# Fourteen unread products ahead of each pair's products with v, and earlier ScalarE copies, in the first stage of an attention and mixing kernel

## The chip, the core and the metric

The kernel runs on one core of one Trainium2 chip. The metric is the device time of one execution in microseconds (us). The core has five engines that run side by side, each through its own list of instructions in order: TensorE (PE, with its weight loads as PEld), VectorE (DVE), ScalarE (ACT), GpSimd (POOL) and SyncE (SP), which issues the transfers. An instruction starts when the one before it on its engine lets it and when the results that it needs are there.

## The reference

Two steps for 8 batches of 576 tokens. First attention with 8 heads of 64 columns, in a causal window of 128 and with a bias that falls with distance; then a block that turns each value by an angle, mixes over the tokens and then over the channels.

```python
scores = scale * np.matmul(q, k.transpose(0, 1, 3, 2))
scores = np.where((rel >= 0) & (rel < 128), scores + bias[None], -1000000000.0)
attn = np.exp(scores - np.max(scores, axis=-1, keepdims=True))
attn = attn / (np.sum(attn, axis=-1, keepdims=True) + 1e-09)
x = concat_heads(np.matmul(attn, v))
theta = x @ w_theta
zr, zi = x * np.cos(theta), x * np.sin(theta)
y = np.einsum('ts,bsd->btd', w_tok_r, zr) + np.einsum('ts,bsd->btd', w_tok_i, zi)
u = x + y
out = u + np.maximum(u @ w_ch, 0.0)
```

## The kernel before

Heads go in pairs, so a batch has four pairs and the kernel 32. A pair passes through these steps. `scores` lets PE make the scores of five tiles in three groups into PSUM (`ps`, two buffers, and `mm`, four buffers); DVE adds the bias and takes the extreme (`weigh`, L433), and ScalarE takes the exponentials (L436). One half of a pair's weights is called `front`, the other `back`. `flip` turns a half so that the keys come to the partitions. For the first four pairs (`PLAIN`) PE turns eight blocks into PSUM and ScalarE copies them out (`pt`, L445). Later pairs are split into two half-precision parts, `hl`, by ScalarE (L450) and DVE (L452), and a transfer turns them (L454). `values` makes the products with v (`ps<-vb,pt` or `ps<-vh,pt`), and `finish` divides by the sums (L483 to L490) into `x_sb`.

The first stage is `start`: pairs 0 to 4, where the scores of a new pair stand between the two flips and the products with v of the pair before. In the same stage ScalarE and DVE unpack the weights (L168 to L193), which arrive as double-precision words, and DVE takes the largest v of each head (L258) and works out scales from it (`spread`, L268 to L288, with two small products on PE). Only pairs 0 to 3 have their products with v in `start`; pair 4 belongs to batch 1.

Then `turn` works out the angles of batch 0: PE turns `x_sb`, ScalarE and DVE cut it into two parts (`x_hi`, `x_lo`), PE multiplies by w_theta (`mm<-wth_hi,x_hi`), and ScalarE and DVE take sine and cosine and split the results (`z_hi` L512, `z_lo` L513). After that `attend` runs the pairs of batch 1 between the token products of batch 0 (`mix`), then `turn` of batch 1 comes, and so on to batch 7.

The order on each engine is fixed when the kernel is built: a scheduler places the instructions by its own picture of time, by the dependencies and by priorities. `tc.high_priority(FINISH)` lets what stands in it go sooner in that order. `tc.issue_after(x)` adds a dependency on x. From the first mix on, PE's products are kept in the order in which they are written (`pinned`); in `start` and `turn` they are not. SP's transfers are ordered by the same scheduler.

Of the kernel before, what the change touches and what calls it, by code (L numbers as in the profile page):

```python
# [11 lines left out]
F32 = mybir.dt.float32  # L12
# [4 lines left out]
BF16 = mybir.dt.bfloat16  # L17
# [16 lines left out]
STEPS, FINISH = ((7, 7, 6, 3), (3, 4, 6, 4), (3, 4, 6, 3)), 250  # L34

GROUP = 4
PLAIN = 4
RINGS = ([("mx", 2 * NT, 4)] + [("den", 2 * NT, 3)] + [("whole", 1, 2), ("vs", 2 * GROUP, 2), ("scale", 2 * GROUP, 2)]
         + [("whole0", 1, 1), ("vs0", 13, 1), ("scale0", 13, 1), ("sum", 9, 1),
# [10 lines left out]
def attn_moe_kernel(ctx: ExitStack, tc: tile.TileContext, qt, kt, vx, wth, wtok, wch, band, out):  # L50
    nc = tc.nc
# [16 lines left out]
    ps_m = ctx.enter_context(tc.tile_pool(name="ps_m", bufs=4, space=PSUM))  # L68
# [3 lines left out]
    def mm(*args, **kw):  # L72
        ins = nc.tensor.matmul(*args, **kw)  # L73
        if pinned:
            tc.keep_in_program_order(ins)

    def behind_all(some):
        stack = ExitStack()
        for ins in some:
            stack.enter_context(tc.issue_after(ins.ins))  # L80
        return stack
# [5 lines left out]
    def flipped(*args):  # L87
        ins = nc.tensor.transpose(*args)  # L88
        if pinned:
            tc.keep_in_program_order(ins)  # L90
# [19 lines left out]
    ident = fixed[:, :128]  # L110
# [16 lines left out]
    sums, rows, invs, lim = (rings[name].take() for name in ("sum", "row", "inv", "lim"))  # L127

    qr = const.tile([128, S + 64], F32, name="qr")
    second = vbp.tile([128, GROUP, NT, 65], F32, name="vb").rearrange("p h c d -> p (h c d)")  # L130
    qr_too, kr_too = second[:, :S + 64], second[:, S + 64:2 * S + 64]
# [110 lines left out]
    def load_plain(g):  # L242
        b, h = divmod(GROUP * g, H)
        vb = vbp.tile([128, GROUP, NT, 65], F32, name="vb")
        nc.sync.dma_start(out=vb, in_=vx[b, h:h + GROUP].rearrange("h p (c d) -> p h c d", d=65))
        return vb
# [3 lines left out]
    def load_values(g):  # L250
        b, h = divmod(GROUP * g, H)
        vb = vbp.tile([128, GROUP, NT, 65], F32, name="vb")
        nc.sync.dma_start(out=vb, in_=vx[b, h:h + GROUP].rearrange("h p (c d) -> p h c d", d=65))
        group_v[g] = vb

    def measure(g, to):

        return nc.vector.tensor_reduce(out=to, in_=group_v[g][:, :, :, :64], axis=mybir.AxisListType.XY, op=ALU.max,  # L258
                                       apply_absolute_value=True)
# [32 lines left out]
    def coming(b):  # L292
        return [g for g in (2 * b + 3, 2 * b + 4) if g < B * H // GROUP]
# [16 lines left out]
    def clamp_first():  # L310
        nc.vector.tensor_scalar(out=peaks[0][:, :H], in0=peaks[0][:, :H], scalar1=2.0 ** -100, scalar2=None,
                                op0=ALU.max)
# [72 lines left out]
    class Pair:  # L385


        def __init__(self, p):
            self.p = p
            self.terms = parts.pop(p)  # L390
            self.early = p < PLAIN
            self.heads = [Head(2 * p + e, self) for e in range(2)]
# [4 lines left out]
        def scores(self, tiles, behind=None):  # L397

            last = len(self.terms) - 1
            if tiles == (0,):  # L400
                _, _, k0, kn, _ = TILES[0]
                ps = ps_m.tile([128, 512], F32, name="mm")
                for j, (qm, km) in enumerate(self.terms):
                    mm(ps[:, :kn], qm[:, 512:], km[:, k0:k0 + kn], start=(j == 0), stop=(j == last))
                self.weigh(0, 0, self.src[0][:, :kn], ps[:, :kn], bands[:, 512:], behind)
                return
            ps = ps_s.tile([128, 2, 512], F32, name="ps")
            if tiles == (1, 2):
                sbs = [self.src[0][:, 256 + 384 * e:640 + 384 * e] for e in range(2)]
            else:  # L410
                self.src[1] = sp.tile([128, 1024], F32, name="back")
                sbs = [self.src[1][:, 512 * e:512 + 512 * e] for e in range(2)]
            off = 0
            for i in tiles:
                q0, qn, k0, kn, _ = TILES[i]
                for j, (qm, km) in enumerate(self.terms):
                    for e in range(2):
                        rows = slice(64 * e, 64 * e + 64)
                        mm(ps[:, e, off:off + kn], qm[rows, q0:q0 + qn], km[rows, k0:k0 + kn],
                                         start=(j == 0), stop=(j == last))  # L420
                off += kn
            off = 0
            for i in tiles:
                _, _, _, kn, c0 = TILES[i]
                for e in range(2):
                    sb = sbs[e][:, off:off + kn]
                    self.weigh(i, e, sb, ps[:, e, off:off + kn], bands[:, 256 * e + c0:256 * e + c0 + kn], behind)
                off += kn
# [9 lines left out]
        def flip(self, half):  # L438
            src = self.src[half]
            if self.early:  # L440
                t_ps = ps_s.tile([128, 2, 512], F32, name="ps").rearrange("p a c -> p (a c)")
                for n in range(8):
                    flipped(t_ps[:, 128 * n:128 * n + 128], src[:, 128 * n:128 * n + 128], ident)
                pt = ptp.tile([128, 1024], F32, name="pt")
                self.copied = nc.scalar.copy(pt, t_ps)  # L445
                parts_of = [pt]
            else:
                hl = hlp.tile([128, 2, 1024], F16, name="hl")
                pt = ptp.tile([128, 2, 1024], F16, name="pt")
                self.copied = nc.scalar.activation(hl[:, 0], src, AF.Copy, scale=2.0 ** PEXP)  # L450
                copied.append(self.copied)
                self.lowered = nc.vector.scalar_tensor_tensor(out=hl[:, 1], in0=src, scalar=2.0 ** PEXP, in1=hl[:, 0],  # L452
                                                              op0=ALU.mult, op1=ALU.subtract)
                nc.sync.dma_start(out=pt.rearrange("p a (n c) -> p (a n) c", c=128),  # L454
                                  in_=hl.rearrange("p a c -> p (a c)"), transpose=True)
                parts_of = [pt[:, a] for a in range(2)]
            for n, (i, e, j) in enumerate(TURNS[half]):
                for to in ((0, 1) if i == 0 else (e,)):
                    at = 128 * n + (64 * to if i == 0 else 0)
                    self.pt[i, to, j] = [t[:, at:at + 128] for t in parts_of]  # L460
# [217 lines left out]
    def prepare(p):  # L678

        if 0 <= p - 1 < pairs and p - 1 not in parts:  # L680
            parts[p - 1] = split_pair(p - 1, raw.pop(p - 1))
        if p < pairs and p not in raw:
            raw[p] = load_pair(p)
# [5 lines left out]
    def attend(b, x_sb, mixing, chans, first, behind, lowered):  # L689

        for g in range(H // 2):
# [15 lines left out]
            for tiles in SCORES:  # L707
                scores(tiles)
# [40 lines left out]
    def start(x_sb, load):  # L749

        paces = [0]

        def pace(k=1):
            for _ in range(k):
                paces[0] += 1
                if paces[0] * 2 % 5 < 2:
                    next(load, None)

        next(load)
        prepare(0)  # L760
        nc.sync.dma_start(out=bands, in_=band)
        prepare(1)
        last = None
        for p in range(H // 2 + 1):
            new = Pair(p)
            if p == 3:
                load_values(2)

            def scores(tiles):
                new.scores(tiles)  # L770
                pace(2 * len(tiles))

            if last is not None:
                last.flip(0)
                scores(SCORES[0])
                scores(SCORES[1])
                last.flip(1)
                scores(SCORES[2])
                last.values()
                with tc.high_priority(FINISH):  # L780
                    last.finish(x_sb)
            else:
                for tiles in SCORES:
                    scores(tiles)
            if p == 3:
                clamp_first()
            if p < H // 2:
                for head in new.heads:
                    head.ready()
            if p in (1, 2):  # L790
                measure(p - 1, peaks[0][:, GROUP * (p - 1):GROUP * p])
            prepare(p + 2)
            last = new
        for _ in load:
            pass
        for g in coming(0):
            load_values(g)
        return last
# [94 lines left out]
```

## Time and profile before

| what | value |
|---|---|
| median of the runs shown | 655.22 us (653.53 to 655.68, 3 runs) |
| the profiled execution's own time | 654.73 us |
| its span from the first to the last instruction | 652.7 us |
| mean granted clock of PE | 0.963 of full speed |
| PE busy | 604.9 us, 93% |
| DVE busy | 529.3 us, 81% |
| ScalarE busy | 499.0 us, 76% |

The span and the execution's own time differ by 2.03 us, which lie around the instructions. The busy shares are means over the whole span; the first stage differs from the rest, so it has to be read by itself. [...]

### The profile page before, as it was taken

What the parts mean: (1) busy time and instruction counts of PE and PEld (TensorE: products, weight loads), DVE (VectorE), ACT (ScalarE), POOL (GpSimd) and SP (SyncE); (2) the same over time, 40 slices, a digit from 0 to 9 for tenths busy, and PEclk for the clock granted to TensorE, in tenths of its full rate; (3) what the DMA queues carried; (4) which work ended last, traced back from release to release, by engine and by line L of the source; (5) the groups of instructions that cost most, each with busy time, mean ns of one, the idle gap of its engine ahead of it and who ended that gap; (6) DMA issues with size and microseconds to landing.
All of it is one profiled execution on the core that took longest, in us unless ns stands there. A gap on an engine that the chain in (4) does not pass through costs nothing.

```text
span 652.7 us, 14918 instructions
## 1 busy us (share of the span) xinstructions
PE 604.9 (93%) x5712; PEld 520.5 (80%) x5712; DVE 529.3 (81%) x1313; ACT 499.0 (76%) x945; POOL 145.7 (22%) x196
## 2 busy tenths in 40 slices
PE   4869888689999999999999999999999999999998
PEld 3758666578887898789878887889878988799887
DVE  4998799797799778988799878997899878946612
ACT  6999879785987668976988778786898799727710
POOL 3001001542213202222203302231212212210220
PEclk9567999798999899999999999999999999999999
DMA  9954412996038740698039920887058901631001
GB/s 267 338 176 123 106 25 59 210 200 147 27 79 199 173 109 21 143 199 188 23 75 197 211 70 20 188 176 171 28 104 197 183 28 41 136 83 38 19 19 56
DMA packets 149096, 79.16 MB, mean 121 GB/s; under 512 B 122144, under 2 KB 138528, under 8 KB 149024
## 3 DMA queue, kind: packets, MB, share of 16 engines
q1 hardware_dynamic: 149024, 78.21, 51.6%
q8 instruction: 45, 0.74, 0.5%
q14 instruction: 27, 0.22, 0.1%
HBM read 39.39 MB, written 9.44 MB: 75 GB/s over the span
## 4 chain that ended last, share of the span: by engine, by line
PE 59%; DVE 18%; ACT 12%; DMA 9%; issue 2%; SPq 0%; POOL 0%; ACTq 0%; DVEq 0%; POOLq 0%
PE mm L73 47%; PE ps L73 9%; DMA pt<-hl 7%; PE ps L88 2%; ACT front L436 2%; ACT back L436 2%; DVE hl L452 2%; DMA qr<-in_qt_dram 2%; ACT hl L450 2%; DVE g L568 1%; DVE f L568 1%; DVE x_sb L490 1%; ACT L436 1%; DVE z_lo L513 1%; DVE fixed L141 1%
## 5 line engine op out<-in xcount | busy, mean ns | idle before, releaser
L73 PE MATMUL mm<-wtk_hi,z_lo 128*128 128x288 f16 x576 | 166.2, 289 | 6.4 <-DVE z_lo L513 5.5
L73 PE MATMUL mm<-wtk_hi,z_hi 128*128 128x288 f16 x576 | 166.8, 290 | 0.5 <-ACT z_hi L512 0.5
L73 PE MATMUL mm<-wtk_lo,z_hi 128*128 128x288 f16 x576 | 166.2, 289 | 0.0
L73 PEld LDWEIGHTS <-z_hi 128*128 128x128 f16 x1152 | 108.1, 99 | 31.1 <-ACT z_hi L512 0.8
L642 POOL TENSOR_TENSOR u_lo<-xtf,u_hi 128x288 fp32r<-128x288 f32 x64 | 54.6, 868 | 137.6 <-DVE vl L370 95.2
L349 POOL TENSOR_TENSOR kl<-kr,kh 128x576 fp32r<-128x576 f32 x31 | 44.0, 1418 | 154.6 <-issue 80.7
L73 PEld LDWEIGHTS <-z_lo 128*128 128x128 f16 x576 | 56.9, 99 | 26.0 <-DVE z_lo L513 10.5
L436 ACT ACTIVATE front<-front,fixed 128x256 f32<-128x256 f32 (+2 forms) x160 | 60.4, 444 | 14.2 <-DVE fixed L433 13.9
L73 PE MATMUL ps<-vh,pt 128*128 128x65 f16 x1008 | 54.6, 198 | 12.6 <-DMA pt<-hl 10.6
L73 PEld LDWEIGHTS <-pt 128*128 128x128 f16 x1512 | 52.7, 100 | 15.3 <-DMA pt<-hl 12.8
L452 DVE SCALAR_TENSOR_TENSOR hl<-front,hl 128x1024 f16<-128x1024 f32 x28 | 51.4, 1837 | 9.4 <-ACT hl L450 9.3
L436 ACT ACTIVATE back<-back,fixed 128x256 f32<-128x256 f32 x128 | 57.2, 494 | 0.4 <-DVE fixed L433 0.4
L640 ACT CAST u_hi<-xtf 128x288 fp32r<-128x288 f32 x64 | 27.0, 423 | 38.9 <-DVE xtf L638 38.9
L73 PE MATMUL ps<-vl,pt 128*128 128x64 f16 x504 | 52.3, 196 | 0.0
L73 PE MATMUL mm<-u_hi,wch_hi 128*128 128x288 f32 x256 | 47.9, 309 | 0.0
L433 DVE CUSTOM_DVE_ANT_0 back<-ps,bands 128x256 f32<-128x256 f32 x128 | 46.8, 419 | 1.1 <-PE ps L73 1.1
L638 DVE SCALAR_TENSOR_TENSOR xtf<-mm,fixed,xtf 128x288 f32<-128x288 f32 x64 | 32.4, 509 | 18.8 <-PE mm L73 18.8
L73 PE MATMUL mm<-wth_hi,x_hi 128*128 128x512 f32 x160 | 46.4, 412 | 0.9 <-DVE x_hi L530 0.9
L73 PE MATMUL ps<-kh,qh 64*128 64x256 f32 (+1 forms) x256 | 41.7, 321 | 5.2 <-DVE x_sb L490 3.9
L670 DVE SCALAR_TENSOR_TENSOR xtf<-mm,xtf 128x288 f32<-128x288 f32 x64 | 29.1, 454 | 20.8 <-PE mm L73 20.0
L73 PE MATMUL mm<-u_hi,wch_lo 128*128 128x288 f32 x256 | 44.5, 295 | 0.0
L73 PE MATMUL mm<-u_lo,wch_hi 128*128 128x288 f32 x256 | 44.4, 295 | 0.0
(162 smaller groups left out, 1487.4 us busy)
## 6 DMA issues: line engine op xcount, KB each, us to landing
vb<-in_vx_dram SPq DMA_DIRECT2D x16, 650.0 KB, 5.7
out_dram<-xtf SPq DMA_DIRECT2D x64, 144.0 KB, 1.8
kr<-in_kt_dram SPq DMA_DIRECT2D x31, 288.0 KB, 3.9
qr<-in_qt_dram SPq DMA_DIRECT2D x31, 144.0 KB, 2.9
qr<-in_qt_dram SPq DMA_DIRECT2D x31, 128.0 KB, 3.1
xtf<-in_wch_dram SPq DMA_DIRECT2D x4, 512.0 KB, 4.2
z_hi<-in_wtok_dram SPq DMA_DIRECT2D x2, 576.0 KB, 6.0
z_lo<-in_wtok_dram SPq DMA_DIRECT2D x2, 576.0 KB, 6.2
```

The source lines that it names most:

```text
L73: ins = nc.tensor.matmul(*args, **kw)
L88: ins = nc.tensor.transpose(*args)
L349: rest = nc.gpsimd.tensor_tensor(out=kl, in0=kr, in1=kh.bitcast(F32), op=ALU.subtract)
L433: self.weighed = nc.vector.tensor_tensor_reduce(out=sb, in0=ps, in1=bias, scale=2.0 ** -(2 * self.p % H + 1), scalar=3.0e38, op0=ALU.add, ...
L436: self.exps.append(nc.scalar.activation(sb, sb, AF.Exp, bias=least, scale=-1.0))
L450: self.copied = nc.scalar.activation(hl[:, 0], src, AF.Copy, scale=2.0 ** PEXP)
L452: self.lowered = nc.vector.scalar_tensor_tensor(out=hl[:, 1], in0=src, scalar=2.0 ** PEXP, in1=hl[:, 0], op0=ALU.mult, op1=ALU.subtract)
L568: nc.vector.scalar_tensor_tensor(out=z, in0=x_sb[:, i, :], scalar=zs[:, c:c + 1], in1=z, op0=ALU.mult, op1=ALU.mult)
L638: nc.vector.scalar_tensor_tensor(out=xtf[:, m, cs], in0=y_ps[:, :HALF], scalar=st["back"], in1=xtf[:, m, cs], op0=ALU.mult, op1=ALU.add)
L640: nc.scalar.copy(u_hi[:, m, cs], xtf[:, m, cs])
L642: return nc.gpsimd.tensor_tensor(out=u_lo[:, m, cs], in0=xtf[:, m, cs], in1=u_hi[:, m, cs].bitcast(F32), op=ALU.subtract)
L670: nc.vector.scalar_tensor_tensor(out=xtf[:, e, cs], in0=o_ps[:, :HALF], scalar=0.0, in1=xtf[:, e, cs], op0=ALU.max, op1=ALU.add)
```

## The change

`unread` makes 14 products of the identity's bits, read as bf16, of 128x128 by 128x256, into an `mm` buffer that nothing reads. They wait for the last scores of the new pair, and the products with v of the pair before wait for them. It happens in four passes of `start`, so 56 products in all. In `flip`, ScalarE's copy of the turned weights now has the priority that `finish` has.

```diff
+UNREAD = 14
...
         ins = nc.tensor.matmul(*args, **kw)
         if pinned:
             tc.keep_in_program_order(ins)
+        return ins
+
+    def unread(behind, n):
+
+        ps = ps_m.tile([128, 512], F32, name="mm")
+        flat = ident.bitcast(BF16)
+        with tc.issue_after(behind.ins):
+            for _ in range(n):
+                behind = mm(ps[:, :256], flat[:, :128], flat, start=True, stop=True)
+        return behind
...
-                        mm(ps[:, e, off:off + kn], qm[rows, q0:q0 + qn], km[rows, k0:k0 + kn],
+                        self.scored = mm(ps[:, e, off:off + kn], qm[rows, q0:q0 + qn], km[rows, k0:k0 + kn],
...
-                self.copied = nc.scalar.copy(pt, t_ps)
+                with tc.high_priority(FINISH):
+                    self.copied = nc.scalar.copy(pt, t_ps)
...
-                last.values()
+                with tc.issue_after(unread(new.scored, UNREAD).ins):
+                    last.values()
```

The scheduler moves more than these lines. The line numbers of the changed kernel are 11 higher in `flip` and 12 higher from `finish` on. The first place is DVE at the end of the first stage, where pair 3 is finished (`x_sb_127`) and pair 4's halves are split (`hl`). Before:

```order
L452 SCALAR_TENSOR_TENSOR hl_787<-front0_101,hl_787 128x1024
L483 TENSOR_SCALAR fixed_100<-ps_670 128x10
L488 RECIPROCAL fixed_100<-fixed_100 128x10
L490 TENSOR_TENSOR x_sb_127<-ps_670,fixed_100 128x2x5x64
L452 SCALAR_TENSOR_TENSOR hl_792<-back_643,hl_792 128x1024
L530 TENSOR_TENSOR x_hi_807<-ps_802,x_hi_807 128x4x64
```

After the change, at the same place:

```order
L464 SCALAR_TENSOR_TENSOR hl_847<-front0_101,hl_847 128x1024
L464 SCALAR_TENSOR_TENSOR hl_852<-back_688,hl_852 128x1024
L495 TENSOR_SCALAR fixed_100<-ps_730 128x10
L279 TENSOR_REDUCE fixed_100<-mm_831 128x1
L500 RECIPROCAL fixed_100<-fixed_100 128x10
L281 TENSOR_SCALAR fixed_100<-fixed_100 128x13
L502 TENSOR_TENSOR x_sb_127<-ps_730,fixed_100 128x2x5x64
L150 TENSOR_SCALAR fixed_100<-mm_835 128x13
...
L157 TENSOR_SCALAR fixed_100<-fixed_100 128x1
L542 TENSOR_TENSOR x_hi_867<-ps_862,x_hi_867 128x4x64
```

The split of pair 4's back half now stands ahead of pair 3's finish, and the scales (`spread`, from L279 on, nine steps from L150 to the second L157) stand between the finish and the first cut of `x_sb`; before, the scales were worked out one pair earlier.

The second place is DVE in `attend` of batch 1, around the split of pair 5's back half (`hl_1070` before, `hl_1130` after). Before:

```order
L490 TENSOR_TENSOR x_sb_990<-ps_1137,fixed_100 128x2x5x64
L370 SCALAR_TENSOR_TENSOR vl_1213<-vb_464,fixed_100,vh_1212 128x320
L141 TENSOR_SCALAR fixed_100<-fixed_100 128x8
L174 SCALAR_TENSOR_TENSOR xtf_797<-xtf_797 128x512
L370 SCALAR_TENSOR_TENSOR vl_1225<-vb_464,fixed_100,vh_1224 128x320
L638 SCALAR_TENSOR_TENSOR xtf_799<-mm_1130,fixed_100,xtf_799 128x288
L433 ISA front0_101,fixed_100<-mm_1260,bands_106 128x192
...
L452 SCALAR_TENSOR_TENSOR hl_1070<-back_1037,hl_1070 128x1024
```

After:

```order
L502 TENSOR_TENSOR x_sb_1050<-ps_1197,fixed_100 128x2x5x64
L381 SCALAR_TENSOR_TENSOR vl_1273<-vb_494,fixed_100,vh_1272 128x320
L185 SCALAR_TENSOR_TENSOR xtf_857<-xtf_857 128x512
L464 SCALAR_TENSOR_TENSOR hl_1130<-back_1097,hl_1130 128x1024
L381 SCALAR_TENSOR_TENSOR vl_1285<-vb_494,fixed_100,vh_1284 128x320
```

The split comes sooner: a piece of v, a step of the token mix and a weighing have moved behind it.

The third place is SP's list at the same point, where the halves of pair 5 are turned. Before:

```order
L454 DMA_TRANSPOSE pt_1066<-hl_1065 128x16x128
L158 DMA xtf_797<-in_wch_dram 128x1024
L253 DMA vb_1238<-in_vx_dram 128x4x325
L454 DMA_TRANSPOSE pt_1071<-hl_1070 128x16x128
L236 DMA qr_119<-in_qt_dram 64x576
```

After:

```order
L466 DMA_TRANSPOSE pt_1126<-hl_1125 128x16x128
L169 DMA xtf_857<-in_wch_dram 128x1024
L466 DMA_TRANSPOSE pt_1131<-hl_1130 128x16x128
L264 DMA vb_1298<-in_vx_dram 128x4x325
L247 DMA qr_119<-in_qt_dram 64x576
```

The load of a group of v has moved from ahead of the second turning transfer to behind it.

## Rows read from the trace of the kernel before

**Rows 1.** By stretch: length; busy PE, PEld, DVE, ACT, POOL; clock, DMA share, GB/s.

```profile
12.50:64.00 51.50, 40.49 (x244) 36.53 (x241) 48.86 (x135) 51.50 (x104) 6.93 (x8) 0.67 0.67 220
64.00:77.25 13.25, 10.06 (x93) 8.95 (x92) 8.98 (x36) 10.97 (x21) 0.00 (x0) 1.00 0.29 71
77.25:103.90 26.65, 23.56 (x140) 17.13 (x140) 24.26 (x38) 21.06 (x36) 0.00 (x0) 1.00 0.24 53
115.50:122.35 6.85, 1.45 (x20) 1.00 (x19) 5.57 (x24) 4.38 (x11) 3.34 (x3) 0.91 1.01 258
148.45:652.70 504.25, 492.06 (x4798) 426.13 (x4798) 402.17 (x975) 371.49 (x701) 114.97 (x154) 0.99 0.49 108
```

**Rows 2.** The same view, cut where PE's granted clock changed.

```profile
18.90:42.40 23.50, 18.48 (x90) 16.77 (x90) 23.10 (x59) 23.50 (x47) 2.88 (x2) 0.50 0.78 264
56.50:120.90 64.40, 52.86 (x454) 42.27 (x454) 57.00 (x159) 53.65 (x100) 7.65 (x11) 1.00 0.34 85
121.60:127.80 6.20, 5.45 (x56) 4.31 (x57) 4.28 (x8) 5.72 (x11) 1.53 (x3) 0.50 0.76 193
```

**Rows 3.** PE in order of time: start, busy us, operation, count, idle before.

```profile
22.82 0.41 PE L73 MATMUL ps<-kh,ql 64*128 64x256 f32 x2
23.03 0.41 PE L73 MATMUL ps<-kl,qh 64*128 64x256 f32 x2
...
24.86 7.94 PE L73 MATMUL ps<-vb,pt 128*128 128x65 f32 x36 [0.32 <-ACT pt L445]
...
60.54 4.23 PE L73 MATMUL ps<-vb,pt 128*128 128x65 f32 x36
...
77.29 1.20 PE L73 MATMUL mm<-wth_hi,x_hi 128*128 128x512 f32 x4 [0.87 <-DVE x_hi L530]
```

**Rows 4.** ScalarE in order of time.

```profile
59.49 1.00 ACT L445 COPY pt<-ps 128x1024 f32<-128x1024 f32 x1
60.38 0.91 ACT L436 ACTIVATE front<-front,fixed 128x256 f32<-128x256 f32 x2
...
65.69 1.01 ACT L445 COPY pt<-ps 128x1024 f32<-128x1024 f32 x1 [1.60 <-PE ps L88]
66.60 1.92 ACT L368 ACTIVATE vh<-vb,fixed 128x320 f16<-128x320 f32 x4
...
74.58 1.06 ACT L450 ACTIVATE hl<-back 128x1024 f16<-128x1024 f32 x1
...
103.28 0.62 ACT L512 CAST z_hi<-f 128x512 f16<-128x512 f32 x1
```

**Rows 5.** DVE in order of time: scales, finish, split and cut.

```profile
66.00 0.16 DVE L139 TENSOR_SCALAR fixed<-mm 128x13 int32<-128x13 int32 x1
...
67.25 0.15 DVE L146 TENSOR_SCALAR fixed<-fixed 128x1 int32<-128x1 int32 x1
...
74.32 0.17 DVE L483 TENSOR_SCALAR fixed<-ps 128x10 f32<-128x10 f32 x1
...
74.77 0.82 DVE L490 TENSOR_TENSOR x_sb<-ps,fixed 128x640 f32<-128x640 f32 x1
75.67 1.23 DVE L452 SCALAR_TENSOR_TENSOR hl<-back,hl 128x1024 f16<-128x1024 f32 x1
76.81 0.42 DVE L530 TENSOR_TENSOR x_hi<-ps,x_hi 128x256 fp32r<-128x256 f32 x1
...
112.95 0.55 DVE L370 SCALAR_TENSOR_TENSOR vl<-vb,fixed,vh 128x320 f16<-128x320 f32 x1
...
114.18 1.33 DVE L452 SCALAR_TENSOR_TENSOR hl<-back,hl 128x1024 f16<-128x1024 f32 x1
```

**Rows 6.** The chain that ended last: start, us, what.

```profile
115.54 6.77 DMA pt<-hl
...
142.12 6.29 DMA pt<-hl
```

**Rows 7.** All 56 turning transfers, from issue to landing.

```profile
DMA to landing us min/median/max: 4.3/5.0/7.3
```

## The prediction

> **What bounds the kernel now.** I read the windows by stage first, then the order in time on PE, ScalarE and DVE where the stages meet, then the chain that ended last. From 148.45 on, PE is busy 492.06 of 504.25 us [rows 1]; neither the code nor the order of PE changes there, so what the change does to the start of that stretch goes through to the end almost whole. Everything turns on the first 148 us. In the first stage ScalarE is the bound: from 12.5 to 64 it is busy 51.50 of 51.50 us, while PE is busy 40.49 and its clock averages 0.67 [rows 1]. After 64 no engine is full until PE starts on w_theta at 77.29 [rows 1, 3]: that tail is a chain of waits. In `turn`, from 77.25 to 103.9, DVE is busy 24.26 of 26.65 us. In batch 1's `attend` the turning transfers are waited for: PE is busy 1.45 us of the 6.85 from 115.5 to 122.35, where a transfer lands after 6.77 us, and another takes 6.29 from 142.12 [rows 1, 6].
>
> **What the clock is worth.** [...] The 36 products with v took 7.94 us at the low level and 4.23 at the high one [rows 3], so pairs 0 and 1, which ran low, could each save 3.71 us of PE, 7.4 together. But what hangs on them in this stage (copies, unpacking, exponentials) is on a ScalarE with no idle time before 64, and it has the same instructions to do: with 51.50 of 51.50 us there is nothing to take out. I count nothing for it. If ScalarE did not cover it, 7.4 us would be the gain.
>
> [...] No run here yet shows what these 14 products do to the clock.
>
> **What the 14 products cost.** Two 64x256 scores side by side follow the pair before at 0.21 us at the low clock (22.82 to 23.03) [rows 3]; an unread product has as many columns, so 14 take 3.0 us, or half, 1.5, at the high clock. The separate weight loads I take as hidden, as they are in the rest of the kernel; the bound from below is nothing for them, the bound from above doubles the 1.5. For pairs 0 and 1 this stands beside the full ScalarE. For pairs 2 and 3 it stands in the chain.
>
> **The tail of the first stage, term by term.** Pair 2's products with v start at 60.54, behind a ScalarE copy that runs from 59.49 [rows 3, 4]. That copy cannot come sooner with the stage full: in the new order two exponentials (0.91 us) have moved ahead of it and one shorter behind, so some 0.4 us later. PE comes to it after turning eight blocks, twelve scores, 14 unread and three more scores: an estimate of 4 us at the high clock and 7.5 at the low one, from a turn that can start only when the copy before has freed the buffer, near 56.5. So pair 2's products start 0.3 to 3 us later; I take 1.2.
>
> From there to pair 4's last split on ScalarE (74.58 plus 1.06 = 75.64) [rows 4] things go both ways: the four conversions of v (1.92 us) have left the way, which helps by at most 0.6 because that stretch waits for PE (1.60 us idle at 65.69) [rows 4]. I take the split 0.4 us later than before, with -0.6 and +2.2 as ends.
>
> Then the new DVE order. Before: pair 3's finish at 74.32 to 75.59, back split 75.67 to 76.90, first cut of `x_sb` 76.81, w_theta products 77.29 [rows 3, 5]: 1.65 us behind the ScalarE split. Now: split 1.23, finish 1.27 and some 0.3 for the two scale steps inside it, then the nine scale steps, which ran from 66.00 to 67.31 (1.3) [rows 5], then the cut, 0.4, and 0.1: 4.6 behind it. That is 2.9 later whatever the clock does. PE's extra products for pair 3 (1.5) hide behind this. The stage thus ends 2.9 + 0.4 = 3.3 us later (2.3 to 5.1).
>
> **`turn` of batch 0.** Three conversions of v (three quarters of 1.92 us [rows 4], 1.4) now stand on ScalarE ahead of the second cut of `x_sb` and of everything behind it; DVE waits for those, and it has only 2.4 us of slack [rows 1]. Nothing behind them hides it: +1.4, between 0 and 2.5. The last `z_hi`, at 103.28 before [rows 4], then comes 4.7 us later in all.
>
> **`attend` of batch 1 gives back.** Three terms. Pair 5's back split moves ahead of a piece of v, a mix step and a weighing, which took DVE from 112.95 to 114.18 [rows 5]: -1.2. Its transfer is now issued ahead of the load of v instead of behind it: it took 6.77 us where the median of all is 5.0 and the least 4.3 [rows 6, 7], so -1.0, between 0 and -2.5. Pair 7's back split likewise moves ahead of its finish and two pieces of v, less a weight step that moved the other way, and its transfer (6.29 us) ahead of a load: -1.5, between 0 and -2.5. What is late next is the split of pair 6, which now stands behind a finish and can cost 0.6, counted in that range.
>
> **Sum.** 3.3 + 1.4 - 1.2 - 1.0 - 1.5 = +1.0 on the profiled execution's 654.73: 655.7 us. That execution lay 0.5 below the runs' median of 655.22. Changes under 0.3% (2.0 us) cannot be told from none here, and my forecast is such a one: **655.7 us, no difference**, between 653.3 and 657.2.
>
> **Rivals.**
>
> *The late stage is not paid back* (slower). If SP's order does not shorten the two transfers, because other traffic fills the queues as well (the DMA share is 1.01 from 115.5 to 122.35 [rows 1]), the 2.5 us of the last two terms go, and PE's longer wait for pair 3's finish can drop the clock ahead of w_theta, where the first four products (1.20 us [rows 3]) would take another 1 us: 654.73 + 1.0 + 2.5 + 1.0 = 659.2. It decides for slower once more than 1.0 us of those 2.5 is missing. For it: the tail's 2.9 us is order alone and sure; against it: the load of v has really moved.
>
> *The clock stays up later on* (faster). The clock fell at 121.5 in PE's wait and was low to 127.8, 6.2 us with PE busy 5.45 [rows 2]. If the shorter transfer shortens that wait, this work takes half, 2.7 us less, and the wait before 148.45, ended the same way, can save 1 more: 655.7 - 3.7 = 652.0. Against it: DVE follows close behind PE there, and part of the wait stays.
>
> [...]
>
> *The 14 products do not lift the clock*: then pair 0's products end some 3 us later (3.0 us more of PE, none saved), the next copy makes ScalarE wait for about 0.8 us, and pair 2's products start 3 us late rather than 1.2: 655.7 + 0.8 + 1.8 = 658.3, slower too. The low clock while PE was busy at 24.86 to 32.8 [rows 2, 3] speaks for it; the dense products here are others.
>
> **Chances.** No difference 0.40. Slower 0.34 (not paid back 0.24, clock not lifted 0.10). Faster 0.26 (clock up later 0.22, early clock reaching the end 0.04). The range that leaves out no more than 2 in 10 runs from 651.5 to 659.5; the signs are close to even, and 653.3 to 657.2 is the range of the likeliest alone.
>
> **What would show it.** Right: ScalarE still full from 12.5 to 64 though pair 0's products take near 4.2 us; w_theta's products starting at 79.5 to 82.5; DVE's back split ahead of the finish, and the nine scale steps between finish and cut; the last `z_hi` near 108; pair 5's turning transfer near 5 to 6 us; PE's long busy stretch beginning at 148.5 to 150.5 instead of 148.45. Wrong: idle time of ScalarE before 64, either way; w_theta at or before 77.3; a low clock in the `turn`; a high clock through 121 to 128.

## The result: 0.6 to 0.7% slower

| | median us (range, runs) | against before, with its 95% interval |
|---|---|---|
| before | 653.53 (652.27 to 656.52, 9) | |
| changed | 658.18 (656.36 to 659.09, 9) | 1.0059 (1.0039 to 1.0079) |
| changed, once more with other runs of before | 658.01 (655.87 to 660.29, 9) | 1.0071 (1.0047 to 1.0096) |

The kernel is 3.9 to 4.6 us slower. The range of the prediction holds that, but the forecast of no difference missed. The profiled execution of the changed kernel took 656.42 us with a span of 654.4.

**The first stage, PE and ScalarE.** The changed kernel's PE in order of time, to compare with [rows 3]:

```profile
22.93 1.70 PE L74 MATMUL mm<-fixed 128*128 128x256 bf16 x14
24.79 4.15 PE L74 MATMUL ps<-vb,pt 128*128 128x65 f32 x36
37.02 0.47 PE L74 MATMUL ps<-kh,qh 64*128 64x128 f32 x2 [7.21 <-ACT pt L457]
...
59.80 1.89 PE L74 MATMUL mm<-fixed 128*128 128x256 bf16 x14
61.84 4.15 PE L74 MATMUL ps<-vb,pt 128*128 128x65 f32 x36
...
70.60 1.70 PE L74 MATMUL mm<-fixed 128*128 128x256 bf16 x14
72.14 4.13 PE L74 MATMUL ps<-vb,pt 128*128 128x65 f32 x36
76.11 0.28 PE L99 MATMUL mm<-fixed,peak 128*128 128x128 f32 x1
...
80.33 1.78 PE L74 MATMUL mm<-wth_hi,x_hi 128*128 128x512 f32 x4 [0.87 <-DVE x_hi L542]
```

Pair 0's 36 products take 4.15 us where they took 7.94. Behind them and the turns of eight blocks PE waits 7.21 us for a copy of ScalarE: what PE saves, it waits. Pairs 2 and 3 gain nothing (4.15 and 4.13 against 4.23), and pay 1.89 and 1.70 for the unread products. w_theta's products start at 80.33, not at 77.29.

ScalarE in order of time, to compare with [rows 4], and the stretches with the columns of [rows 1]:

```profile
59.56 0.98 ACT L457 COPY pt<-ps 128x1024 f32<-128x1024 f32 x1
...
75.05 1.06 ACT L462 ACTIVATE hl<-back 128x1024 f16<-128x1024 f32 x1
...
108.47 0.62 ACT L524 CAST z_hi<-f 128x512 f16<-128x512 f32 x1
```

```profile
12.50:64.00 51.50, 38.00 (x268) 32.75 (x267) 48.13 (x131) 51.24 (x104) 6.72 (x8) 0.80 0.69 219
...
152.00:654.40 502.40, 489.40 (x4812) 423.99 (x4809) 402.21 (x978) 372.79 (x706) 117.94 (x156) 1.00 0.51 109
```

ScalarE is as full before 64 as it was (51.24 of 51.50), with a higher mean clock. Its copy for pair 2 stands at 59.56 against 59.49: the clock bought nothing there. (The 0.67 and 0.80 of these rows do not compare: the changed kernel's clock record begins only at 22.67, and time before that reads as 1.00. From 22.70 to 64, where both traces have a record, the mean is 0.64 before and 0.75 after.) The last `z_hi` comes at 108.47 (before: 103.28).

**The end of the stage.** DVE in order of time, to compare with [rows 5]:

```profile
76.14 1.22 DVE L464 SCALAR_TENSOR_TENSOR hl<-back,hl 128x1024 f16<-128x1024 f32 x1 [1.38 <-ACT hl L462]
77.28 0.16 DVE L495 TENSOR_SCALAR fixed<-ps 128x10 f32<-128x10 f32 x1
...
77.82 0.81 DVE L502 TENSOR_TENSOR x_sb<-ps,fixed 128x640 f32<-128x640 f32 x1
78.55 0.16 DVE L150 TENSOR_SCALAR fixed<-mm 128x13 int32<-128x13 int32 x1
...
79.86 0.41 DVE L542 TENSOR_TENSOR x_hi<-ps,x_hi 128x256 fp32r<-128x256 f32 x1
```

The order is the one foreseen: back split, finish, scale steps, cut. The back split cannot start before ScalarE's own, so DVE waits 1.38 us there while PE ends pair 3's products (at 76.27) and the finish could soon begin.

**A low clock in the turn.** The columns of [rows 1] again, over the stretches with a low granted clock, in the first and in the second trace of the changed kernel:

```profile
101.40:108.00 6.60, 6.35 (x39) 5.05 (x40) 5.70 (x10) 5.92 (x12) 0.00 (x0) 0.50 0.01 1
```

```profile
101.50:107.50 6.00, 6.00 (x39) 4.73 (x39) 5.10 (x9) 5.36 (x11) 0.00 (x0) 0.50 0.00 1
```

Ahead of it PE waits, in the first trace, in the order of the rows 1.62, 0.31, 0.63 and 0.61 us for `z_hi` and `z_lo`. Scores and mixing products then run at a granted clock of 0.50. Pair 4's products, which stand behind them, start 4.6 us after the last `z_hi` starts (113.05) and 4.7 in the second trace, where three traces with the order of before have 3.2 each. That is PE's delay; whether it costs time is taken up with the give-back below.

### The profile page after: what moved, and what is told of

Same layout as the page of the kernel before. It is cut to its first block, busy times and chain, and to the rows that moved or that the text cites. A ratio compares the mean times of both kernels' runs of the same rounds, so it can differ in the third digit from the quotient of the medians.

```text
span 654.4 us, 15032 instructions
## 1 busy us (share of the span) xinstructions
PE 606.2 (93%) x5768; PEld 520.8 (80%) x5768; DVE 528.9 (81%) x1313; ACT 498.0 (76%) x945; POOL 145.7 (22%) x196
## 4 chain that ended last, share of the span: by engine, by line
PE 61%; DVE 15%; ACT 12%; DMA 9%; issue 2%; SPq 1%; POOL 0%; ACTq 0%; DVEq 0%; POOLq 0%
PE mm L74 48%; PE ps L74 10%; DMA pt<-hl 5%; DMA qr<-in_qt_dram 3%; PE ps L99 3%; ACT front L447 2%; ACT back L447 2%; DVE hl L464 2%; DVE z_lo L525 2%; ACT hl L462 2%; DVE g L580 1%; DVE f L580 1%; DVE x_sb L502 1%; ACT L447 1%; DVE fixed L152 1%
## 5 line engine op out<-in xcount | busy, mean ns | idle before, releaser
L74 PE MATMUL ps<-vh,pt 128*128 128x65 f16 x1008 | 53.0, 196 | 10.9 <-DMA pt<-hl 10.3
L74 PEld LDWEIGHTS <-pt 128*128 128x128 f16 x1512 | 51.0, 99 | 13.8 <-DMA pt<-hl 11.8
L652 ACT CAST u_hi<-xtf 128x288 fp32r<-128x288 f32 x64 | 27.1, 423 | 37.2 <-DVE xtf L650 37.2
L74 PE MATMUL ps<-kh,qh 64*128 64x256 f32 (+1 forms) x256 | 43.4, 335 | 12.4 <-ACT pt L457 7.2
L74 PE MATMUL ps<-vl,pt 128*128 128x64 f16 x504 | 50.7, 194 | 0.0
L74 PE MATMUL mm<-wth_lo,x_hi 128*128 128x512 f32 x160 | 44.6, 401 | 0.0
```

The costliest lines, as they stand in the source:

```text
L652: nc.scalar.copy(u_hi[:, m, cs], xtf[:, m, cs])
```

## Experiments

All ratios are against runs of the kernel before on the same chip. The intervals are of 95%.

**The priority alone.**

```diff
-                with tc.issue_after(unread(new.scored, UNREAD).ins):
-                    last.values()
+                last.values()
```

> Only the priority of ScalarE's copies, without the 14 products. The order of the instructions is the same as in the kernel before on every engine, so every theory expects no difference: a ratio of 1.000 within 0.002. It also shows how far two equal programs lie apart in such a comparison.

Measured: 1.0002 (0.9979 to 1.0025). The second half of the change does nothing: "copies sooner" is not what happens. It does nothing beside the products either: the changed kernel, built without it, has the same instructions in the same order on every engine. The whole new order comes from the scheduler's picture of 14 more products.

**Half of the pairs.** Pairs 0 and 1 alone, then 2 and 3 alone (`p` is the new pair, one ahead):

```diff
-                with tc.issue_after(unread(new.scored, UNREAD).ins):
                 # pairs 0 and 1
+                with tc.issue_after(unread(new.scored, UNREAD if p < 3 else 0).ins) if p < 3 else nullcontext():
                 # pairs 2 and 3
+                with tc.issue_after(unread(new.scored, UNREAD).ins) if p > 2 else nullcontext():
```

> The 14 products only in front of the products with v of pairs 0 and 1. Here DVE's nine scale steps keep the place of before, and only pair 4's back split still moves ahead of pair 3's finish. Order theory (the loss is DVE's new order at the end of the first stage): w_theta starts about 1.3 us later than before, and the kernel is 1 us slower (1.0015 to 1.002). Rival (the loss is PE's own time for the 14 products in front of pairs 2 and 3): as the kernel before, 1.000. Should the early high clock be worth something, faster, down to 0.989 (7.4 us).

> The 14 products only in front of the products with v of pairs 2 and 3. DVE's order at the end of the first stage is that of the changed kernel (split, finish with scale steps, the other scale steps, cut), and the order of batch 1's transfers is that of before. Order theory: w_theta 2.9 us later, the turn another 1.5 to 2 us, so 1.006 to 1.007, as much as the whole change. Rival (PE's own time): w_theta 1.5 to 3.4 us later with DVE waiting for PE, 1.003 to 1.005; both put the loss in this half, and the idle time ahead of DVE's cut tells which it is.

Measured: 1.0124 (1.0091 to 1.0158) and 1.0091 (1.0062 to 1.0121). Each half costs at least as much as the whole, so they do not add. For pairs 0 and 1 the loss is far beyond both theories (1.000 to 1.002); for pairs 2 and 3 the order theory's 1.006 to 1.007 lies within the interval. With pairs 2 and 3, w_theta starts at 81.89 and the last `z_hi` at 110.32; SP's order is that of before, so nothing is given back. The eight microseconds of pairs 0 and 1 are taken up below.

**The order alone, and the products without it.** Pair 4's back split on DVE is held behind pair 3's finish, as before the change, with all products and then with those of pairs 2 and 3 only; and DVE's new order is made without any product.

```diff
 # all products, or those of pairs 2 and 3
-                self.lowered = nc.vector.scalar_tensor_tensor(
+                with behind_all(finished if half else ()):
+                    self.lowered = nc.vector.scalar_tensor_tensor(
...   # (the arguments, as before)
 # no products: finish and scales behind the split
+    with tc.issue_after(first[-1].lowered.ins), tc.high_priority(FINISH):
+        done = held.pop().finish(x_sb)
+    with tc.issue_after(done.ins), tc.high_priority(FINISH):
+        scales_first()
```

> The changed kernel with all 14 products, but DVE's back split of pair 4 is held behind pair 3's finish, as in the kernel before; the scale steps then fall behind the cut of x_sb for the most part. Order theory: w_theta at 77.5 to 78.5 instead of 80.33, and most of the loss is gone: 1.000 to 1.002 against the kernel before. Rival (PE's own time for the products): w_theta stays near 80 because the finish itself is late, and the ratio stays near 1.005.

> The 14 products only in front of the products with v of pairs 2 and 3, with DVE's back split of pair 4 held behind pair 3's finish. Against the run with these products alone (1.0091) only the order differs. Order theory: most of that loss goes, 1.001 to 1.003. Rival (PE's own time): the finish waits for PE, w_theta still starts 2 to 4 us late, and the ratio stays between 1.004 and 1.009.

> No unread products and the kernel before everywhere else, but at the end of the first stage DVE does pair 4's back split first, then pair 3's finish, then the first four scale steps, then the cut of x_sb; the four conversions of v move behind the cut on ScalarE too. PE has no extra work. Order theory: the cut comes 1.2 to 1.9 us later behind ScalarE's split, w_theta starts near 79, and the kernel is slower by as much: 1.002 to 1.003. Rival (all of the loss is PE's own time for the products and its clock): 1.000.

Measured: 1.0029 (1.0005 to 1.0053) with all products, 1.0054 (1.0033 to 1.0074) with those of pairs 2 and 3, 1.0046 (1.0018 to 1.0074) for the order alone. The order alone costs about 3.0 us without products (1.2 to 4.8). That order is a neighbour of the changed kernel's and not the same: only four of the scale steps stand ahead of the cut, and PE puts two of their products ahead of w_theta. Putting the finish first takes 0.30 and 0.42 points off the two measurements of the changed kernel and 0.37 off the run with pairs 2 and 3; each of these ratios is known to 0.2 or 0.3 points. So the order theory holds in part. Its sign in the trace did not come: with all products and the finish first, w_theta should have started at 77.5 to 78.5 and started at 80.89. The rival holds beside it: with the finish first, the products ahead of pairs 2 and 3 still cost 3.5 us (2.2 to 4.8), along with what else of the order has moved. In that run DVE waits for PE:

```profile
78.18 0.17 DVE L496 TENSOR_SCALAR fixed<-ps 128x10 f32<-128x10 f32 x1 [1.55 <-PE ps L74]
...
80.71 0.41 DVE L543 TENSOR_TENSOR x_hi<-ps,x_hi 128x256 fp32r<-128x256 f32 x1
```

**What the early clock is worth by itself.** Products for pairs 0 and 1 again, with both of DVE's splits of pair 4 in the order of before.

```diff
+                with behind_all(finished if half else kept and [self.weighed]):
+                    self.lowered = nc.vector.scalar_tensor_tensor(
...   # (the arguments, as before)
```

> The 14 products only in front of the products with v of pairs 0 and 1, and at the end of the stage DVE keeps the order of the kernel before (front split behind pair 4's last weighing, pair 3's finish ahead of the back split). It asks what the early clock is worth by itself. If ScalarE covers it, as the prediction counted: 1.000. If it reaches the end: down to 0.989 (7.4 us), or in part, 0.995 to 0.998, since pair 2 came 0.3 us late in the changed kernel and 1 to 2 us late with products for pairs 2 and 3 alone. Rival from the run with these products and the other order (1.0124): the clock's low stretch falls into the chain of waits after 60 us instead, pair 2's products take some 6 us instead of 4.2, and the kernel is slower, 1.004 to 1.008.

Measured: 1.0071 (1.0048 to 1.0095): the rival. PE and ScalarE of this run, and the stretch behind pair 2's start:

```profile
62.29 6.52 PE L74 MATMUL ps<-vb,pt 128*128 128x65 f32 x36 [1.30 <-DVE fixed L444]
```

```profile
70.56 1.01 ACT L457 COPY pt<-ps 128x1024 f32<-128x1024 f32 x1 [5.90 <-PE ps L99]
```

```profile
66.00:72.00 6.00, 6.00 (x36) 5.97 (x35) 2.27 (x11) 1.44 (x3) 0.00 (x0) 0.50 0.20 58
```

Pairs 0 and 1 ran at 4.15 and 4.23 us. But PE waits 1.30 us ahead of pair 2's products, and then the clock is low from some 64 to 74 us, in the chain of waits: 6.52 instead of 4.23 us, and ScalarE waits 5.90 us for PE where it waited 1.60 [rows 4]. The run with these products and the other order has the same low stretch (6.06 us, a wait of 5.36). In the twelve other traces the clock is high from 64 to 72. That low stretch is where the early products alone lose. It is missing in the four traces that have products ahead of all pairs, so those ahead of pair 2 seem to keep it away; that is read from the traces, and no run isolates it.

**The give-back by itself.** No products; SP's loads of v in batch 1 behind the back transfers, then the same with ScalarE's conversions of v moved as well, then, in the kernel with all products and the finish first, the one load of pair 5 moved and nothing else.

```diff
-                load_values(2 * b + 3 + g // 2)
+                with tc.issue_after(new.sent.ins) if b == 1 else nullcontext():
+                    load_values(2 * b + 3 + g // 2)
...
 # conversions of v, in the second of the three only
-                with tc.issue_after(st[0]["split"].ins):
+                with behind_all([st[0]["split"], done_hl]):
                     waiting.pop(0).ready()
```

> The kernel before without any products; only SP's two loads of v in batch 1 are put behind the back transfers of pairs 5 and 7 (ScalarE and DVE reorder a little behind that, from pair 6 on). It is the give-back of the prediction by itself. If the transfers get shorter by 1.0 us each as counted there, and PE waits less for them: 0.996 to 0.998. Rival (the transfer is as long as other traffic makes it, or pair 6 becomes late instead): 1.000.

> No products. Both moves of the changed kernel that the runs speak for: SP's two loads of v behind the back transfers (0.9962 alone), and ScalarE's four conversions of v (1.92 us) behind pair 4's back split instead of ahead of its first exponentials; DVE's and PE's order in the first stage is that of before. Order theory: pair 4's split on ScalarE comes up to 0.9 us earlier, the conversions then stand ahead of the second cut of x_sb and take that back in part: 0.994 to 0.996. Rival: the conversions cost more behind the split than they did ahead (the prediction's 1.4 us in the turn): 0.998 or more.

> The kernel with all 14 products and pair 3's finish ahead of pair 4's back split (1.0029), and one row of SP changed: batch 1's load of v stands behind pair 5's back transfer instead of ahead of it. If the shorter transfer is given back to the end here too, as it was without products (0.9962 for two loads): 1.001 or less, and pair 5's products start 5.3 to 5.8 us behind the issue instead of 7.5. Rival (in this order pair 6's exponentials on ScalarE are late next and take it): 1.003 with the same shorter transfer.

Measured: 0.9962 (0.9937 to 0.9986), 0.9966 (0.9945 to 0.9987) and 0.9998 (0.9978 to 1.0018). The moved loads of pairs 5 and 7 give 2.5 us (0.9 to 4.1) without products; the other engines' orders shift a little too from pair 6 on. In the last pair of kernels exactly one row of SP has moved, and the ratio goes from 1.0029 to 0.9998; each is against its own runs of before, and the difference of 0.31 points is about as large as its uncertainty. The conversions add nothing. SP in order of time, first with the load ahead (finish first), then behind:

```profile
119.41 0.38 SPq L264 DMA_DIRECT2D vb<-in_vx_dram  x1
119.89 5.36 SPq L467 DMA_TRANSPOSE pt<-hl  x1
```

```profile
118.58 3.52 SPq L467 DMA_TRANSPOSE pt<-hl  x1
122.15 0.58 SPq L264 DMA_DIRECT2D vb<-in_vx_dram  x1
```

Pair 5's products on these blocks start 7.5 us behind the issue in the first (127.36) and 5.5 in the second (124.06). The kernel before with the loads behind, without or with the conversions, is the only one here that is faster than before.

**Activity in the wait of `attend`.** The 14 products behind the scores of pair 6, none in the first stage.

```diff
+            if b == 1 and g == 1:
+                unread((new or pair).scored, UNREAD)
             pair.values()
```

> The kernel before without products in the first stage; 14 unread products stand in batch 1 behind the scores of pair 6, where PE waits for pair 5's transfer (115.5 to 122.35). The order on DVE, ScalarE and SP is that of before. If PE's activity in that wait holds the clock up, the low stretch from 121.5 to 127.9 goes, 2.7 us less: 0.996. Rival: the products end long before the transfer lands and the clock falls in the rest of the wait: 1.000.

Measured: 1.0014 (0.9995 to 1.0032), so no gain. The clock is still low in its trace, from some 126 to 129 us, and so for about half as long as the 6.2 us of [rows 2]; it does not reach the end.

**The changed kernel again** (no edit).

> The changed kernel once more, for a second trace of it beside the same runs of before. The ratio should be near 1.006. What the first trace shows of order has to come again: ScalarE's pair 6 exponentials some 18.4 us behind the last z_hi instead of 16.1, pair 5's products 5.8 us behind the issue of its transfer. What only the clock did in that one execution need not: the low clock at w_theta's first products (80.8 to 84.1), in the mixing products at 101.4 to 108, and at 138.9 to 145.3. If the low stretch in the mixing products comes again, it belongs to the change (PE waits for z_lo there) and costs 1.3 us.

Measured: 1.0071, as in the first section. The low stretches in w_theta's first products and in the mixing products came again; the first trace's stretch at 138.7 to 145.6 did not, and one at 124.9 to 131.8 came in its place.

## Why the prediction missed

The sum was 3.3 + 1.4 - 3.7 = +1.0, made against one trace of before. Three traces have the order of before (before, the priority alone, the filled wait, which differs only by its products on PE). Their mean stands against that of the two traces of the changed kernel:

| us | before, 3 traces | changed, 2 traces | difference | predicted |
|---|---|---|---|---|
| w_theta's first product starts | 77.29, 78.23, 78.10 | 80.33, 80.01 | +2.3 | +3.3 |
| from there to the last `z_hi` | 25.99, 27.41, 27.54 | 28.14, 28.00 | +1.1 | +1.4 |
| to pair 7's last product with v | 47.41, 47.11, 46.29 | 45.16, 44.55 | -2.1 | -3.7 |
| to batch 1's first turning of `x_sb` | 4.88, 6.07, 5.01 | 5.70, 6.65 | +0.9 | 0 |
| to the end of the span | 497.13, 492.88, 493.86 | 495.07, 496.09 | +1.0 | 0 |

These rows make +3.1, and the runs 3.9 to 4.6. In the last row the order is the same in all five, and the values overlap; that part, and the 1 us or so that the traces leave open, is not located.

- **Clock, counted as nothing.** Right for what it bought, and of the rival that the products do not lift the clock the forecast is out (3 us more of PE, none saved): in six traces with products ahead of pairs 0 and 1 pair 0's 36 products take 4.15 us, in eight without them 5.71 to 7.95. The low and the high level are the 0.50 and the 1.00 of [rows 2]. What is shown is that the clock stays up, and not that the unread products raise it: in the changed kernel's two traces it rose 0.26 and 0.11 us before the first of them started (in the first trace two 64x256 scores side by side stand 0.21 us apart up to 22.54, two unread products 0.11 apart from 23.05 on), in the four others up to 2.7 us after; and in four of the eight traces without them it rose at 23.4 to 23.9 too, but fell again within pair 0's products, at 26.8 to 27.4. The changed kernel first, then the filled wait, which has none here (columns of [rows 1]):

```profile
22.70:32.90 10.20, 7.12 (x67) 6.59 (x63) 9.72 (x24) 10.19 (x21) 0.00 (x0) 1.00 0.99 302
```

```profile
23.65:27.00 3.35, 2.84 (x25) 2.64 (x23) 3.35 (x8) 3.35 (x7) 0.00 (x0) 1.00 1.05 405
27.05:44.05 17.00, 11.39 (x59) 9.62 (x58) 16.73 (x44) 17.00 (x36) 1.47 (x1) 0.50 0.59 180
```

The early clock did not reach the end because ScalarE was full (51.24 of 51.50 us); PE waited 7.21 us instead. The prediction's 7.4 us of gain, for a ScalarE that did not cover it, did not come: the trace shows that the clock was high, and not that the time follows.
- **The 14 products, 1.5 or 3.0 us.** They took 1.70 to 1.89 us at the high clock and 3.17 in pair 1 at the low one. Right.
- **The tail, +3.3.** Within its bounds (2.3 to 5.1): +3.0 against the one trace that it was worked out from, and +2.3 against three, because that trace was 0.9 ahead of the two others. The order term was a little large: from the end of ScalarE's split to w_theta it is 1.65, 1.64 and 1.65 us before and 4.22 and 4.23 in the changed kernel, so 2.6 and not 2.9. The split itself ends 0.3 us sooner against three traces, where 0.4 later was counted. The 3.0 us of the order alone do not confirm the 2.9, since that run has another order. "PE's extra products for pair 3 hide behind this" holds only while the order is as it is. With the finish first they show, 1.55 us of waiting in the row above, and of the 2.6 us only 1.0 comes back (3.19 to 3.20 in three traces).
- **`turn`, +1.4.** +1.1, so the size is right. That the conversions of v are its cause is not shown: no run moves them alone to this place, and the low clock from 101 to 108 lies in the same stretch.
- **The give-back, -3.7: here the sum failed, in its first term.** Only 2.1 us came back. That term, -1.2 for pair 5's back split, gave nothing: its transfer is issued 12.29 and 12.48 us behind the last `z_hi` in the changed kernel, and 12.26, 12.25 and 12.26 in the three traces of before. DVE and SP before, then changed:

```profile
109.13 1.78 DVE L452 SCALAR_TENSOR_TENSOR hl<-front,hl 128x1024 f16<-128x1024 f32 x1
115.54 4.71 SPq L454 DMA_TRANSPOSE pt<-hl  x1
```

```profile
113.66 0.28 DVE L279 TENSOR_REDUCE fixed<-mm 128x1 f32<-128x128 f32 x1
...
114.28 1.19 DVE L281 TENSOR_SCALAR fixed<-fixed 128x8 f32<-128x8 f32 x1
115.32 1.21 DVE L464 SCALAR_TENSOR_TENSOR hl<-front,hl 128x1024 f16<-128x1024 f32 x1
...
119.13 1.22 DVE L464 SCALAR_TENSOR_TENSOR hl<-back,hl 128x1024 f16<-128x1024 f32 x1
...
120.32 0.34 SPq L169 DMA_DIRECT2D xtf<-in_wch_dram  x1
120.76 3.73 SPq L466 DMA_TRANSPOSE pt<-hl  x1
```

The back split does stand closer to the front split, 3.8 us from start to start where it was 5.05 (114.18 in [rows 5]). But the front split starts 6.85 us behind the last `z_hi`, where it was 5.85: a third `z_lo` and two steps of `spread` now stand ahead of it. And SP issues the transfer 0.41 us behind the split's end, after a load of weights, where it was 0.03. The sum counted what had moved behind the back split, and not what had moved ahead of the front one.

The second term, -1.0 for the transfer, was right and a little small: pair 5's products start 5.8 and 5.6 us behind its issue in the changed kernel (126.53 and 120.76 in the first trace), against 6.8 to 7.3 with the load ahead, so -1.4. The third, -1.5 for pair 7, gave 0.8: from pair 5's products to pair 7's last it is 27.1 and 26.5 us, against 28.3, 27.6 and 26.7. The kernel with the finish first and the load behind needs 43.47 us for the whole stretch, 3.5 less than before, so there was that much to have.

The later start of pair 4's products (3.0 us behind the last `z_hi` there, 4.6 and 4.7 here) does not explain the loss. DVE is full from the last `z_hi` to the end of the back split, before and changed, so a faster PE would not have brought that split forward, although PE is full there too after the change. The chain that ended last runs over DVE there in both traces of the changed kernel. Before, then changed:

```profile
103.28:115.51 12.23, 11.63 (x143) 9.40 (x144) 12.22 (x40) 11.81 (x23) 3.48 (x5) 1.00 0.43 97
```

```profile
108.47:120.35 11.88, 11.88 (x151) 10.10 (x150) 11.81 (x34) 10.42 (x20) 1.47 (x2) 1.00 0.36 85
```

So "a low clock in the `turn`", a sign that was to show the prediction wrong, came in both traces, and no run shows that it costs anything behind the `turn`.
- **Behind the give-back, nothing counted.** Here is what became late next. PE of the changed kernel's second trace, behind pair 7's products (151.30 is the transfer that the prediction wanted shorter):

```profile
151.30 0.20 PE L74 MATMUL ps<-vh,pt 128*128 128x65 f16 x1 [1.25 <-DMA pt<-hl]
155.47 0.40 PE L74 MATMUL mm<-u_hi,wch_hi 128*128 128x288 f32 x1 [1.22 <-ACT wch_hi L207]
156.83 0.40 PE L74 MATMUL mm<-u_hi,wch_lo 128*128 128x288 f32 x1 [0.57 <-POOL wch_lo L208]
```

The wait for the transfer, 3.24, 2.30 and 2.70 us in the three traces of before, is 1.25 here and gone in the first trace. The sign that PE's long busy stretch begins at 148.5 to 150.5 did not come: the products behind this wait, at 148.45 before, start at 151.30 in the second trace. Two waits for pieces of the channel weights take 1.79 us, and the first trace has one of 0.81; the chains go back from there over POOL and ScalarE. Such waits (0.8 to 1.8 us in all) stand in all six traces that have pair 7's load behind its transfer, with unread products or without, and in none of the eight others. So they belong to the moved load. The +0.9 of the table is no more than this points to: its values overlap (5.70 changed, 6.07 before).

One suspicion fell. Pair 6's four exponentials stand on ScalarE behind a longer wait for such a piece, in the changed kernel and then in the filled wait:

```profile
124.67 0.68 ACT L179 ACTIVATE xtf<-xtf 128x512 f32<-128x512 f32 x1 [2.53 <-DMA xtf<-in_wch_dram]
...
126.83 1.48 ACT L447 ACTIVATE front<-front,fixed 128x128 f32<-128x128 f32 x4
```

```profile
121.23 0.67 ACT L179 ACTIVATE xtf<-xtf 128x512 f32<-128x512 f32 x1 [1.51 <-DMA xtf<-in_wch_dram]
121.80 1.48 ACT L447 ACTIVATE front<-front,fixed 128x128 f32<-128x128 f32 x4
```

They start 18.4 us behind the last `z_hi` there (126.83 and 108.47), and 16.2 here (121.80 and 105.64). But the kernel with the finish first and the load behind has 17.4 and still comes out level with before, and of the changed kernel's two chains only one goes over this wait. So this is not the main part.

So the range held by errors of both signs: the tail and `turn` cost 1.3 us less than counted, the give-back was 1.6 short, and 1.9 came from behind it.

Of the rivals, "the late stage is not paid back" gave the sign and the size (+4.5 forecast, 3.9 to 4.6 measured) by luck, with the wrong reason: it expected the transfers to stay long. They got shorter, but the first of them was not issued sooner. Its other half, a low clock at w_theta's first products, came (1.78 us for four, against 1.20), but two of the three traces with the order of before show it too (2.08 and 1.97).

"The clock stays up later on" had named a high clock through 121 to 128 as its sign. That came in the first trace, where the clock was high from 108.0 to 138.7; the low stretch had moved (138.7 to 145.6, and 124.9 to 131.8 in the second trace) and was not gone, and the kernel was slower. That the early clock reaches the end, with its chance of 0.04, is out, as the bullet on the clock says.

## What to carry to other kernels

Here pair 0's products went from 7.94 us at a clock of 0.50 to 4.15 at 1.00, and PE then waited 7.21 us for a copy of a full ScalarE: where the clock is higher, look at what PE does right after the faster stretch. If a scheduler works from its own picture of time, even unread work reorders every engine; measure the order alone and the work alone, and expect that halves of such a change do not add. A transfer that a queue issues ahead of a waited-for one is worth moving by itself: here two such moves gave 2.5 us, and the rest of the change spent it. When an instruction moves sooner in a list, look also at what has moved ahead of the one before it.

## What the hardware showed

The record of the granted clock can begin late, and what lies before it reads as 1.00. The first record stands at 15.29 in the trace of before, at 22.67 in the changed kernel's and only at 43.83 in that of the priority alone. In the last, pair 0's 36 products took 7.95 us in a stretch that reads 1.00:

```profile
25.00 7.95 PE L74 MATMUL ps<-vb,pt 128*128 128x65 f32 x36 [0.32 <-ACT pt L457]
```

```profile
25.00:32.50 7.50, 7.50 (x35) 7.50 (x36) 7.50 (x20) 7.50 (x17) 0.00 (x0) 1.00 1.00 296
```

That 1.00 is no reading. In the same trace two scores side by side stand 0.21 us apart up to 43.60, as at the low clock in [rows 3], and 0.13 behind the first record (43.81 to 43.94). In the trace of before the same products took 7.94 us at a recorded 0.50, in the changed kernel 4.15 at a recorded 1.00. So the low clock, which the prediction took for the cause of the 7.94, stands; and the share of a stretch is worth looking at only behind the first change of level in the trace.

Executions of one order differ in where the low stretches fall. The last `z_hi` starts at 103.28, 105.64 and 105.64 in the three traces with the order of before, and the whole spans of those (652.7, 651.7 and 650.8) do not follow it. Of a prediction worked out from one trace, a term of 1 or 2 us at a fixed place is therefore within what two executions differ by.
